# The left half of eight output chunks stored from GpSimd's queue, behind the last weights

## The chip, the core, the metric

The kernel runs on one core of a Trainium2 chip. The metric is device microseconds for one launch, median of several runs. PE is TensorE, DVE VectorE, ACT ScalarE, POOL GpSimd, and SP SyncE. DMA queue q0 takes what GpSimd issues, q1 what SP issues.

## The reference

Attention with four batches, eight heads, 768 positions and 64 features per head, some heads causal over everything, others with four sink positions and a window of 64. Its output, seen as 3072 rows of 512, goes into a mixture of eight experts with soft slots, four to an expert:

```python
logits = x @ phi                                  # 3072 x 32
d = softmax(logits, over rows)                    # dispatch
slot_input = (d.T @ x).reshape(8, 4, 512)
for e in range(8):
    slot_out[e] = relu(slot_input[e] @ w1[e]) @ w2[e]     # 512 -> 1024 -> 512
out = softmax(logits, over slots) @ slot_out      # 3072 x 512
```

All inputs and the output are float32; w1 and w2 are 2 MB for each expert.

## The kernel before

The program is one straight list of instructions. Attention runs over pairs of heads in an order written out by hand (ORDER), in which the loads of the weights are placed between the loads of q, k and v. All these loads are issued by GpSimd, since they cast float32 to bfloat16 on the way (w_load, w2_half). The second matrices of experts 5, 6 and 7 share their memory with the buffers of q, k, v and of the masks. So they come last, in halves of 256 output columns, left half (c = 0) and right half (c = 1), in this order:

```python
w_load(NE + 4)                 # expert 4, whole
w2_half(5, 0); w2_half(6, 0); w2_half(7, 0)
w2_half(5, 1); w2_half(6, 1); w2_half(7, 1)
```

After attention come the experts. `first` and `turn_h` make the hidden layer; `second(es, cols)` adds the products of the given experts for the left or right columns into one of two PSUM banks, `spb[0]` and `spb[1]` (L666). When the left bank is whole, VectorE scales it into the left half of `slot_out` (L742); ScalarE does the same for the right half (L751).

The 3072 output rows are twelve chunks of 256. For the first NL chunks the left half is computed before the right weights have come: `half_rows(i, 0)` makes two matmuls (L718), and evicts with VectorE (even chunks, L726) or with two ScalarE instructions (odd chunks, L724) into the tile `ot`, of which there are twelve buffers. `store` (L704) then issues a DMA on SP; for half a chunk it moves 256 KB in rows of 1 KB. When the right half of `slot_out` is there, `half_rows(i, 1)` follows for the NL chunks. The remaining chunks are made whole by `full_rows` (L734, L737, L739), with one store of 512 KB each.

`stir(c)` issues c matmuls of 128x448 whose result nobody reads (L678), so that TensorE has something to do while it waits for weights. TensorE takes its instructions in order, so that every product of `second` waits for the landing of its own weights and holds up what is behind it.

A DMA's issuing engine waits for the data that it moves, and for the earlier DMA that used the same completion count. There are eight such counts for GpSimd's DMAs and eight for SP's, used in turn.

Of the kernel before, what the change touches and what calls it, by code (L numbers as in the profile page):

```python
# [329 lines left out]
def kernel(  # L330
# [13 lines left out]
    nc = tc.nc  # L344
# [4 lines left out]
    NE, DM, F = moe_w1.shape  # L349
# [275 lines left out]
    def bank(i, shape, dt=F32):  # L625

        return tps.tile(shape, dt, tag=f"b{i}", name=f"b{i}")
# [28 lines left out]
    def second(es, cols, last=False):  # L656

        n = 4 // len(es)
        for c in cols:
            if c not in spb:  # L660
                spb[c] = bank(HP[6 + c], [P, 256])
        for f in range(8 // n):
            for x in range(4):
                e, fo = es[x // n], 8 // n * (x % n) + f
                for c in cols:
                    nc.tensor.matmul(spb[c][32 * x:32 * (x + 1), :], hTs[e // 4][:, fo, 32 * (e % 4):32 * (e % 4) + 32],  # L666
                                     w2s[e][:, fo, 256 * c:256 * (c + 1)],
                                     start=(x, c) not in begun, stop=last and f == 8 // n - 1)
                    begun.add((x, c))
# [3 lines left out]
    def stir(c):  # L673

        if not awake:
            awake.append(bank(HP[5], [P, 448]))
        for _ in range(c):
            nc.tensor.matmul(awake[0], ident, w1s[0][:, 0, :448], start=True, stop=True)  # L678
# [16 lines left out]
    second((7,), (0,), last=True)  # L695

    chunks = [(b, c) for b in range(B) for c in range(3)]
    NL = 7
    ots = {}

    def store(i, c0, c1):
        b, c = chunks[i]
        ov = out[b * S + 256 * c:b * S + 256 * (c + 1), :].rearrange("(p r) d -> p r d", r=2)
        nc.sync.dma_start(ov[:, :, c0:c1], ots[i][:, :, c0:c1])  # L704

    free = HP[:5]

# [4 lines left out]
    def half_rows(i, c):  # L712
        b, ch = chunks[i]
        if i not in ots:
            ots[i] = osb.tile([P, 2, DM], F32, tag="ot", name="ot")
        op = out_bank([P, 2, 256])
        for r in range(2):
            nc.tensor.matmul(op[:, r, :], out_rows(b, ch, r), slot_out[:, 256 * c:256 * (c + 1)],  # L718
                             start=True, stop=True)
        o = ots[i][:, :, 256 * c:256 * (c + 1)]  # L720
        rr = rrow[:, b, 2 * ch:2 * ch + 2]
        if i % 2:
            for r in range(2):
                nc.scalar.activation(o[:, r, :], op[:, r, :], ACT.Copy, scale=rr[:, r:r + 1])  # L724
        else:
            nc.vector.tensor_mul(o, op, rr.rearrange("p (r o) -> p r o", o=1).to_broadcast([P, 2, 256]))  # L726
        store(i, 256 * c, 256 * (c + 1))

    def full_rows(i):
        b, ch = chunks[i]  # L730
        ots[i] = osb.tile([P, 2, DM], F32, tag="ot", name="ot")
        for r in range(2):
            op = out_bank([P, 512])
            nc.tensor.matmul(op, out_rows(b, ch, r), slot_out, start=True, stop=True)  # L734
            rr = rrow[:, b, 2 * ch + r:2 * ch + r + 1]
            if r:
                nc.scalar.activation(ots[i][:, 1, :], op, ACT.Copy, scale=rr)  # L737
            else:
                nc.vector.tensor_scalar_mul(ots[i][:, 0, :], op, rr)  # L739
        store(i, 0, DM)  # L740

    nc.vector.tensor_scalar_mul(slot_out[:, :256], spb[0], rcol)  # L742
    for i in range(NL):
        if i == 4:
            second((5,), (1,))
        half_rows(i, 0)
        stir(1)
    second((6,), (1,))
    stir(4)
    second((7,), (1,), last=True)  # L750
    nc.scalar.activation(slot_out[:, 256:], spb[1], ACT.Copy, scale=rcol)  # L751
    for i in range(NL):
        half_rows(i, 1)
    for i in range(NL, len(chunks)):
        full_rows(i)
# [35 lines left out]
```

## Time and profile before

| | |
|---|---|
| median of 3 runs | 152.34 us (152.04 to 152.39) |
| the profiled execution's time | 152.27 us |
| its span, first to last instruction | 150.4 us |
| mean granted TensorE clock | 0.953 |
| busy: PE, DVE, ACT, POOL | 87%, 76%, 69%, 24% |
| q0 (GpSimd): packets, MB, share of 16 engines | 13104, 26.22, 92.8% |
| q1 (SP): packets, MB, share of 16 engines | 5248, 6.37, 12.2% |
| stores of half a chunk | 14 of 256 KB |
| stores of a whole chunk | 5 of 512 KB |

Times in the views are microseconds from the start of the span. In the rows of 40 digits each digit is a busy share in tenths for a fortieth of the span (or of the window asked for). The DMA share is that of the core's 16 DMA engines together; packets overlap, so it can be over 1. MB of q0 are counted as written, in bfloat16; twice as much is read. A matmul group's line gives its start, its length, and in brackets the idle time before it and what ended that.

### The profile page before, as it was taken

What the parts mean: (1) busy time and instruction counts of PE and PEld (TensorE: products, weight loads), DVE (VectorE), ACT (ScalarE), POOL (GpSimd) and SP (SyncE); (2) the same over time, 40 slices, a digit from 0 to 9 for tenths busy, and PEclk for the clock granted to TensorE, in tenths of its full rate; (3) what the DMA queues carried; (4) which work ended last, traced back from release to release, by engine and by line L of the source; (5) the groups of instructions that cost most, each with busy time, mean ns of one, the idle gap of its engine ahead of it and who ended that gap; (6) DMA issues with size and microseconds to landing.
All of it is one profiled execution on the core that took longest, in us unless ns stands there. A gap on an engine that the chain in (4) does not pass through costs nothing.

```text
span 150.4 us, 5249 instructions
## 1 busy us (share of the span) xinstructions
PE 130.2 (87%) x2321; PEld 84.1 (56%) x2321; DVE 114.7 (76%) x258; ACT 103.6 (69%) x139; POOL 36.2 (24%) x69
## 2 busy tenths in 40 slices
PE   6979999999999999999999999889799998439500
PEld 2436677676677677667757676556564745125100
DVE  4869899999969999998999998899933506208700
ACT  3029989999899999998989987999134104117700
POOL 6634231141137004025920000830530000000000
PEclk9999999999999999999999999999999999965955
DMA  2999999999999999999999999999999999975996
GB/s 24 200 207 208 209 228 201 215 227 201 211 224 203 216 224 196 227 207 203 227 212 213 222 216 216 213 211 218 220 206 192 198 199 197 300 263 187 356 403 251
DMA packets 18374, 32.91 MB, mean 219 GB/s; under 512 B 1712, under 2 KB 11440, under 8 KB 16688
## 3 DMA queue, kind: packets, MB, share of 16 engines
q0 software_dynamic: 13104, 26.22, 92.8%
q1 hardware_dynamic: 5248, 6.37, 12.2%
q8 instruction: 18, 0.29, 0.7%
q14 instruction: 4, 0.03, 0.1%
HBM read 52.50 MB, written 6.29 MB: 391 GB/s over the span
## 4 chain that ended last, share of the span: by engine, by line
PE 42%; DMA 20%; ACT 14%; DVE 13%; issue 2%; POOL 1%; POOLq 1%; ACTq 0%
DMA w<-in_moe_w_dram 16%; PE sc L166 11%; ACT pT L174 11%; PE pv L208 9%; DMA w<-in_k_dram 4%; DVE pT L193 4%; DVE xb L222 3%; PE tpv L120 3%; PE tpx L231 3%; PE tpk L120 3%; PE lgs L255 3%; PE tpq L120 2%; PE tpb L138 2%; PE b L718 2%; PE zp L422 1%
## 5 line engine op out<-in xcount | busy, mean ns | idle before, releaser
L174 ACT ACTIVATE pT<-sc 128x1024 bf16<-128x1024 f32 (+1 forms) x96 | 81.2, 928 | 5.4 <-PE sc L166 4.9
L193 DVE TENSOR_TENSOR pT<-pT,w 128x1024 bf16<-128x1024 bf16 (+2 forms) x64 | 33.0, 531 | 2.6 <-ACT pT L174 2.5
L166 PE MATMUL sc<-qT,kT 64*128 64x512 bf16 (+3 forms) x256 | 32.6, 309 | 1.7 <-ACT pT L174 1.0
L208 PEld LDWEIGHTS <-pT 128*128 128x128 bf16 x672 | 25.0, 97 | 9.5 <-issue 7.2
L208 PE MATMUL pv<-vb,pT 128*128 128x65 bf16 x352 | 28.5, 194 | 0.1
L120 PEld LDWEIGHTS <-w 96*64 96x64 bf16 x768 | 19.0, 111 | 9.6 <-issue 6.2
L208 PE MATMUL pv<-vf,pT 128*128 128x65 bf16 x320 | 24.3, 194 | 0.0
L222 DVE TENSOR_TENSOR xb<-pv,rs 128x768 bf16<-128x768 f32 (+1 forms) x17 | 15.5, 910 | 0.6
L166 PEld LDWEIGHTS <-kT 64*128 64x128 bf16 x256 | 10.4, 93 | 9.8 <-issue 3.7
L264 POOL COPY expT<-ep 128x128 bf16<-128x128 bf16 x18 | 6.8, 430 | 21.9 <-ACT ep L260 21.9
L724 ACT ACTIVATE ot<-b,rrow 128x256 f32<-128x256 f32 x12 | 5.0, 471 | 10.0 <-PE b L718 9.5
L726 DVE TENSOR_TENSOR ot<-b,rrow 128x512 f32<-128x512 f32 x8 | 5.5, 692 | 8.2 <-PE b L718 8.0
L153 DVE TENSOR_TENSOR vf<-vb,fmask 128x528 bf16<-128x528 bf16 x16 | 11.2, 697 | 0.0
L103 POOL DMA_DIRECT2D w<-in_k_dram x8 | 5.1, 643 | 19.3 <-PE sc L166 12.3
L422 PE MATMUL zp<-w 128*128 128x512 bf16 x23 | 8.5, 502 | 1.2 <-DVE quarter L425 1.2
L236 DVE COPY xT<-tpx 128x768 bf16<-128x768 bf16 x16 | 8.7, 549 | 0.7 <-PE tpx L231 0.7
L120 PE MATMUL tpk<-ident,w 96*64 96x96 bf16 x256 | 8.3, 208 | 1.0 <-DMA w<-in_k_dram 1.0
L231 PE MATMUL tpx<-ident,xb 128*128 128x128 bf16 x96 | 8.0, 218 | 1.0 <-DVE xb L222 0.8
L103 POOL DMA_DIRECT2D w<-in_q_dram x8 | 5.4, 672 | 14.1 <-PE tpq L120 13.2
L666 PE MATMUL b<-w,hT 128*32 128x256 bf16 x128 | 5.2, 283 | 3.9 <-DMA w<-in_moe_w_dram 3.9
L132 DVE COPY kT<-tpk 128x768 bf16<-128x768 bf16 x14 | 7.6, 549 | 1.2 <-PE tpk L120 1.2
L132 DVE COPY qT<-tpq 128x768 bf16<-128x768 bf16 x15 | 8.0, 549 | 0.7 <-PE tpq L120 0.7
(110 smaller groups left out, 168.5 us busy)
## 6 DMA issues: line engine op xcount, KB each, us to landing
w<-in_moe_w_dram POOLq DMA_DIRECT2D x13, 1024.0 KB, 17.9
out_dram<-ot SPq DMA_DIRECT2D x14, 256.0 KB, 4.8
w<-in_q_dram POOLq DMA_DIRECT2D x8, 384.0 KB, 12.4
w<-in_k_dram POOLq DMA_DIRECT2D x8, 384.0 KB, 10.5
w<-in_v_dram POOLq DMA_DIRECT2D x8, 384.0 KB, 10.9
w<-in_moe_w_dram POOLq DMA_DIRECT2D x6, 512.0 KB, 20.3
out_dram<-ot SPq DMA_DIRECT2D x5, 512.0 KB, 4.9
phf<-in_moe_phi_dram SPq DMA_DIRECT2D x4, 16.0 KB, 8.4
```

Of the source, the lines that this page charges most:

```text
L103: self.nc.gpsimd.dma_start(self.raws[t][Q % 2][:96], s)
L120: self.nc.tensor.transpose(tp[64 * hp:64 * hp + 64, x, :], raw[:96, hp, s * 64:s * 64 + 64], self.ident[:96, :96])
L132: self.nc.vector.tensor_copy(o, i)
L153: self.nc.vector.tensor_mul(vf, self.vbs[n // 2 % 2][:, n % 2, :, :4, :], fm.to_broadcast([128, 2, 4, VW]))
L166: nc.tensor.matmul(sc[:, hh, o:o + w], kT[ps, (g0 + j) * 128:(g0 + j + 1) * 128], qT[ps, g0 * 128 + q0:g0 * 128 + q0 + w], start=True, sto ...
L174: self.nc.scalar.activation(self.pT[n][:, :, lo:hi], self.sc.pop((n, u))[:, :, :hi - lo], ACT.Exp, scale=self.scale)
L193: nc.vector.tensor_mul(v, v, m)
L208: self.nc.tensor.matmul(pv[:, i * 65:(i + 1) * 65], pT[:, hh, o:o + 128], (vb if i - j <= 1 else vf)[:, j, :65], start=(j == 0), stop=(j = ...
L222: nc.vector.tensor_mul(x[:, hs], pv[:, :, :, :64], rs[:, :c].to_broadcast([128, c, 6, 64]))
L231: self.nc.tensor.transpose(tp[:, i * 128:(i + 1) * 128], self.xb[b][:, i, n4 * 128:(n4 + 1) * 128], self.ident)
L236: self.nc.vector.tensor_copy(self.xT[n // 4][:, n % 4], self.tp.pop(("x", n, 0)))
L422: nc.tensor.matmul(zp[:, i % 2, :], zw[:, :128], zw, start=True, stop=True)
```

## The change

Eight chunks instead of seven have their left half made ahead. Their left stores are issued by GpSimd and no longer by SP, after GpSimd's last weights; right halves and whole chunks stay on SP. So there are 8 left stores from GpSimd, and 8 right and 4 whole ones from SP. Four unread products are put ahead of expert 6's right product, and seven instead of four stand between it and expert 7's.

```diff
-    NL = 7
+    NL = 8
     ots = {}
 
     def store(i, c0, c1):
         b, c = chunks[i]
         ov = out[b * S + 256 * c:b * S + 256 * (c + 1), :].rearrange("(p r) d -> p r d", r=2)
-        nc.sync.dma_start(ov[:, :, c0:c1], ots[i][:, :, c0:c1])
+
+        (nc.gpsimd if c1 < DM else nc.sync).dma_start(ov[:, :, c0:c1], ots[i][:, :, c0:c1])
...
             second((5,), (1,))
         half_rows(i, 0)
         stir(1)
+    stir(4)
     second((6,), (1,))
-    stir(4)
+    stir(7)
     second((7,), (1,), last=True)
```

## The prediction

> **What bounds the kernel now.** I read the profile page first, then the chain that ended last, then the transfers and the busy times in short stretches of the last 30 us, since the change touches nothing before the left half of the output. On the page the DMA row is full to the end but for one hole, just where the clock row falls:
>
> ```profile
> PEclk9999999999999999999999999999999999965955
> DMA  2999999999999999999999999999999999975996
> GB/s 24 200 207 208 209 228 201 215 227 201 211 224 203 216 224 196 227 207 203 227 212 213 222 216 216 213 211 218 220 206 192 198 199 197 300 263 187 356 403 251
> ```
>
> The chain of waits says who stands around that hole (start, length, what):
>
> ```profile
> 109.44 24.01 DMA w<-in_moe_w_dram
> 133.49 0.64 PE b L666 x7
> 134.16 0.48 ACT slot_out L751
> 134.68 3.14 PE b L718 x14
> ```
>
> The last weights, right half of expert 7's second matrix, were issued at 109.44 and landed at 133.45. Only then come the product, the right half of slot_out, and the right stores. The left stores, which need none of this, are issued by SP from 125.98 on. The busy times by stretch, whose last columns are the clock, the DMA share and GB/s, show what that does:
>
> ```profile
> 126.00:128.00 2.00, 2.00 (x22) 1.12 (x19) 1.36 (x2) 1.53 (x5) 0.00 (x0) 1.00 1.46 198
> 130.00:132.00 2.00, 0.37 (x2) 0.09 (x1) 0.00 (x0) 0.00 (x0) 0.00 (x0) 1.00 1.12 351
> 132.00:133.50 1.50, 0.01 (x3) 0.01 (x2) 0.00 (x0) 0.00 (x0) 0.00 (x0) 0.85 0.95 325
> 133.50:135.00 1.50, 0.93 (x10) 0.48 (x10) 0.00 (x0) 0.47 (x1) 0.00 (x0) 0.50 0.62 220
> 135.00:136.00 1.00, 1.00 (x7) 0.67 (x5) 0.69 (x1) 0.27 (x1) 0.00 (x0) 0.50 0.20 70
> 136.00:137.00 1.00, 1.00 (x7) 0.67 (x6) 0.69 (x1) 0.99 (x4) 0.00 (x0) 0.50 0.04 15
> 145.00:149.20 4.20, 0.00 (x0) 0.00 (x0) 0.00 (x0) 0.00 (x0) 0.00 (x0) 0.50 0.97 383
> ```
>
> Three things are to be seen. The DMA engines, full until 133, run dry before the first right store arrives. Taking 1.00 as full, the idle part is 0.05 x 1.5 + 0.38 x 1.5 + 0.80 + 0.96, and half of 137.0 to 137.5: 2.64 us of all 16 engines. They don't run dry together: a share of 0.20 is three engines, 0.04 less than one. And from 137.2 to the last packet at 149.2 they are full again, so the end is set by bytes. Besides, the stores squeeze the weights; the queues from 131 to 132 (packets, MB, share):
>
> ```profile
> q1 hardware_dynamic: 369, 0.36, 104.9%
> q0 software_dynamic: 11, 0.01, 4.1%
> ```
>
> q0, the GpSimd queue, still has a trickle of weights on a few late engines, while q1, SP's, has the rest. On the late engines stores and weights take turns, and the right product waits for the latest.
>
> **The change part by part.** The sum is made against the profiled execution: span 150.4, time 152.27, so 1.87 lies around the span; the median is 152.34, 0.07 more.
>
> *Weights first.* The eight left stores (c1 is 256, under DM) go into q0 behind all weights. Expert 6's right half landed at 129.1 (the wait before its product ended at 129.11), when stores had hardly begun. A half is 0.52 MB, at 198 GB/s 2.65 us. So expert 7's lands at about 131.75 instead of 133.45: 1.7 us earlier.
>
> *From landing to the first right store.* Before: 133.49 to 136.02, SP's issue, and first packets at 137.2, 3.7 us. Expert 7's product took 0.62 and the first output pair, to its eviction, 0.62 too (134.68 to 135.30), in a stretch with clock 0.50; at clock 1.00 the left ones took 0.40 and 0.41 (124.85 to 125.26). That saves 0.4 if TensorE stays awake, so first right packets at 131.75 + 3.3 = 135.05. These 2.1 us are worth only what the DMA queues leave of them.
>
> *Unread products.* The eighth left chunk adds a pair and one unread product, 0.41 by the step of its neighbours; four unread products took 0.86, seven make 1.43. From 128.23, where TensorE was done with seven chunks: 128.64, 129.50 after four, 129.85 after expert 6's right product (landed at 129.1, so 0.4 late, which nobody waits for), 131.3 after seven. Expert 7 lands at 131.75: cost nothing. If it landed at 130.7, they would cost 0.6 on the right product, still behind left stores. The bound is 0 to 0.6; I take 0.
>
> *GpSimd's issues.* GpSimd has no work after 110.3. Its issues took 0.54 to 0.90, SP's 0.58; eight follow the evictions, from 126.0 on. The order of the changed kernel shows more: each store takes the next of eight completion counts, so stores 6, 7 and 8 also wait for the right halves of experts 5, 6 and 7. The first two have landed by then. The eighth can be issued at 131.75 only, and with 0.9 of issue and 1.2 until packets (SP's 136.02 to 137.2) starts at 133.9. At 126.0 q0 had 1359 packets of weights left, which at the 386 a us of 120 to 124 are gone by 129.5 on the mean engine; seven stores of 0.70 then last to 134.4, so it isn't missed; only behind an early engine is there a gap. Nothing is queued on GpSimd behind it.
>
> The Trainium skill, "DMA: Bandwidth & Descriptors", section "SWDGE vs HWDGE vs iDMA", speaks against this: GpSimd writes its descriptors into SBUF, where VectorE in its two-port mode locks it out. By that the issues could stretch. The trace of before doesn't show it: two weight issues at 72.82 took 1.08 together while VectorE was over nine tenths busy.
>
> *Rate of the stores in q0.* The trace has no store there. From above: q1's 1 KB packets, 370 in a us on 16 engines, 43 ns each, up to 46.5 with all busy (344 GB/s, 138 to 140): 0.69 to 0.75 a store, 16 packets an engine. From below: the weights' packets also read 1 KB, 1024 in 2.65 us on 16 engines, 41 ns. The worst row is the time of one q0 packet from 120 to 124: 143.9% of 16 engines x 4 us over 1545 packets is 59.6 ns, but these overlap. I take 0.70 a store, the range 0.66 to 0.95.
>
> *SP.* Seven issues leave its queue, and one 512 KB store becomes two of 256 KB, one on each queue. A full store costs 1.29 (0.524 MB at 405 GB/s, 143.5 to 149), a half one on SP 0.76 (0.262 MB at 344): two halves 0.70 + 0.76, 0.17 more.
>
> *The sum.* If all engines fill their hole, 2.64 - 0.17 = 2.5 us are won. The latest engine has less to win: its left packets ended at about 136.55 (where the share goes to zero), so it was idle for 0.65. It then has the eighth left store, 0.70, until 137.25, eight right ones of 0.76 and four full of 1.29: 148.5. Before, the last packets were at 149.2. That is 0.7 won. Why it is late: expert 7's left half landed at 122.74 (issued 106.84, 15.9 to landing); two halves later is 128.04, but expert 6's right half landed at 129.1, 1.06 late. Between them, before 124, q8 fetched instructions once; q8's 18 packets with 0.7% of 16 engines x 150.4 us are 0.94 us each, on one engine. Before, the hole absorbed this lateness; now it doesn't. But a late engine works while others have finished, at 43 ns a packet, not 46.5: 8 x 16 x 3.5 ns = 0.4 of the right stores. I take 1.1, nearer to the latest engine than to the mean: every store needs all 16. Time: 152.27 - 1.1 = 151.2.
>
> **The rivals.** *Engines even out* (0.17): lateness is recovered, since early engines idle while late ones catch up. For it: 4% and 20% in the hole are few engines; against it: the late one's 1.06 at 129.1 is more than one whole fetch. 152.27 - 2.5 = 149.8.
>
> *Order without gain* (0.13): weights and stores interleave as before and expert 7 still lands at 133.45. Left stores then end before 137.2 on most engines all the same, and only the eighth chunk's half is won: after 137.2 eight x 0.76 + four x 1.29 instead of seven and five, 0.53 less: 151.7. Against it: from 115 to 126, with weights alone, q0 ran at an even 198 GB/s in order. The Trainium skill says in the same page, "Issuing engines are not separate DMA queues", that choosing another issuing engine only saves issue time; by that alone I would have said 0 won. The same page, "Queues, rings and completion order", has rings of one queue taken in order, which is what the rest of my case needs.
>
> *Slower* (0.14): q0's store packets take the whole 59.6 ns instead of 43. Eight stores x 16 packets x 16.6 ns = 2.1 us, on every engine, between the weights and the right stores, so nothing hides it: 152.27 - 1.1 + 2.1 = 153.3. It decides from 43 + 1100 / 128 = 52 ns a packet. For it: the row stands there; against it: the same row moves a packet each 41 ns. A late issue on GpSimd would have the same sign, but needs stores 3 us late.
>
> **How the numbers follow.** Forecast 0.56, the three rivals 0.44. This kernel can be told from no change at 0.3%, 0.46 us. Faster takes most of the forecast (0.48; the rest falls within, as its own bounds are 150.6 to 151.9), the evened case (0.17) and some of the third (0.05): 0.70. Within: 0.16. Slower: 0.14. The range reaches from 150.0, short of the evened end, to 152.6, into the slow case.
>
> **What would show it.** Right: expert 7's wait ends near 131.75; the DMA share stays about 1 from 130 to 149; q1 starts at about 135; the chain names stores and not weights; the last packets near 148.1, spread over engines. Wrong: a share under 0.9 between 131 and 136 (stores issued late or slow); left stores landing more than 0.8 apart in q0; expert 7 landing at 133 or later; unread products standing right before its product.

## The result, and the profile after

The changed kernel took 151.39 us (median of 20 runs, 150.72 to 152.84) against 152.36 for the kernel before (20 runs): ratio 0.9955, 95% interval 0.9933 to 0.9976. That is 0.97 us by the medians, 0.36 to 1.02 by the interval; forecast were 151.2 and 1.1.

The profiled execution of the changed kernel was one of the long ones (152.84, span 151.1), and it was long before the change begins: VectorE scaled the left half of slot_out at 126.20, against 124.31 in before. So times of the two profiles are not laid side by side here; I count from landmarks, events that both traces have. The chain of waits of the changed kernel (start, length, what):

```profile
111.32 22.78 DMA w<-in_moe_w_dram
...
134.14 0.42 PE b L666 x8
...
134.59 0.48 ACT slot_out L753
...
135.12 0.61 PE b L719 x4
```

From the left scaling to the end of the wait for expert 7's right weights it is 7.94 us, where it was 9.18. The busy times by stretch (the last three columns are the clock, the DMA share, GB/s):

```profile
132.00:133.50 1.50, 1.12 (x6) 0.48 (x5) 0.00 (x0) 0.00 (x0) 1.16 (x2) 1.00 1.08 348
133.50:135.00 1.50, 0.40 (x8) 0.22 (x8) 0.00 (x0) 0.41 (x1) 0.35 (x1) 1.00 1.01 379
135.00:136.00 1.00, 0.88 (x9) 0.79 (x9) 0.47 (x1) 0.32 (x2) 0.33 (x1) 1.00 0.79 303
136.00:137.00 1.00, 1.00 (x10) 0.68 (x8) 1.00 (x3) 1.00 (x4) 0.00 (x0) 1.00 0.74 275
137.00:137.50 0.50, 0.38 (x4) 0.18 (x2) 0.50 (x2) 0.50 (x2) 0.00 (x0) 1.00 0.25 98
145.00:149.20 4.20, 0.00 (x0) 0.00 (x0) 0.00 (x0) 0.00 (x0) 0.00 (x0) 0.50 0.93 370
```

The hole in the DMA share is smaller, 0.21 + 0.26 + 0.75 x 0.5 = 0.85 us of 16 engines instead of 2.64, but it is not closed. GpSimd's and SP's issues in the timeline (start, length, and in brackets the idle time before and what ended it):

```profile
128.14 5.02 POOL L705 DMA_DIRECT2D out_dram<-ot  x7 [15.95 <-DVE ot L727]
134.65 0.69 POOL L705 DMA_DIRECT2D out_dram<-ot  x1 [1.49 <-DMA w<-in_moe_w_dram]
136.25 9.37 SPq L705 DMA_DIRECT2D out_dram<-ot  x12
```

The eighth left store did wait 1.49 for the weights, as the order of completion counts said. SP's first right store came 2.11 after the end of expert 7's wait, where it was 2.53. Last, what GpSimd's stores look like on the queue: q0 had 13104 packets before.

```profile
q0 software_dynamic: 13744, 28.31, 96.8%
q1 hardware_dynamic: 3472, 4.27, 8.2%
```

640 packets more for eight stores are 80 each, for 256 KB: 64 of 4 KB and 16 short ones, not 1 KB rows one by one as on q1.

One thing stood in no term of the forecast. From the last landing to the end of the span it was 0.91 in before, 1.35 here. The waits of SP (line, what it waited for: total, times, longest), in before and then in the changed kernel:

```profile
SPq L786 <- DMA out_dram<-ot: 3.2, 3, 1.2
```

```profile
SPq L788 <- DMA out_dram<-ot: 4.0, 1, 4.0
```

At the end SP goes through its completion counts one after the other, in a fixed order, some 0.06 us each even when they are full (in the changed kernel's trace its last waits follow the last landing at steps of 0.06 us). In before the last three stores end three waits in turn, and the last store's count is the last in the order. With 12 stores on SP instead of 19 the last store falls on the first of the eight counts: one wait of 4.0, and all the others still to be gone through behind the last landing.

### The profile page after: what moved, and what is told of

Same layout as the page of the kernel before. It is cut to its first block, busy times and chain, and to the rows that moved or that the text cites. A ratio compares the mean times of both kernels' runs of the same rounds, so it can differ in the third digit from the quotient of the medians.

```text
span 151.1 us, 5272 instructions
## 1 busy us (share of the span) xinstructions
PE 129.4 (86%) x2329; PEld 84.1 (56%) x2331; DVE 113.6 (75%) x257; ACT 104.0 (69%) x142; POOL 42.0 (28%) x77
## 4 chain that ended last, share of the span: by engine, by line
PE 47%; DMA 20%; ACT 19%; DVE 3%; issue 3%; POOL 2%; ACTq 0%; POOLq 0%
DMA w<-in_moe_w_dram 15%; PE sc L166 14%; ACT pT L174 13%; PE pv L208 11%; DMA w<-in_k_dram 5%; PE tpv L120 4%; PE tpx L231 3%; PE tpq L120 3%; PE tpk L120 3%; PE tpb L138 3%; PE lgs L255 3%; ACT ot L725 2%; PE zp L422 2%; DVE xb L222 1%; ACT ot L738 1%
## 5 line engine op out<-in xcount | busy, mean ns | idle before, releaser
L208 PEld LDWEIGHTS <-pT 128*128 128x128 bf16 x672 | 24.9, 97 | 9.3 <-issue 7.1
L725 ACT ACTIVATE ot<-b,rrow 128x256 f32<-128x256 f32 x16 | 6.3, 480 | 9.5 <-PE b L719 9.1
L705 POOL DMA_DIRECT2D out_dram<-ot x8 | 5.7, 1081 | 17.4 <-DVE ot L727 15.9
L120 PE MATMUL tpq<-ident,w 96*64 96x96 bf16 x256 | 8.1, 209 | 1.0 <-DMA w<-in_q_dram 1.0
L120 PE MATMUL tpv<-ident,w 96*64 96x96 bf16 x256 | 8.7, 216 | 0.0
## 6 DMA issues: line engine op xcount, KB each, us to landing
w<-in_moe_w_dram POOLq DMA_DIRECT2D x13, 1024.0 KB, 16.9
```

Of the source, the lines that this page charges most:

```text
L120: self.nc.tensor.transpose(tp[64 * hp:64 * hp + 64, x, :], raw[:96, hp, s * 64:s * 64 + 64], self.ident[:96, :96])
L208: self.nc.tensor.matmul(pv[:, i * 65:(i + 1) * 65], pT[:, hh, o:o + 128], (vb if i - j <= 1 else vf)[:, j, :65], start=(j == 0), stop=(j = ...
```

## The experiments

To compare executions that reach the end at different times, I use one more landmark of each trace: the mean of the 16 engines' landings of expert 7's left half, which no store touches. "Wait" is from there to the end of the wait for expert 7's right half, "rest" from the end of that wait to the end of the span, "SP" from it to SP's first right store, "last" from the last landing to the end. "Stage", in the texts below, is from VectorE's scaling of the left half of slot_out to the end of the span: 26.1 in before, 24.9 in the changed kernel. The trace gives the 16 landings of each DMA without the engines' names; "the latest engine" is the last of the 16.

| kernel | time, us | ratio (95%) | wait | rest | SP | last |
|---|---|---|---|---|---|---|
| before | 152.36 | | 11.74 | 16.96 | 2.53 | 0.91 |
| after | 151.39 | 0.9955 (0.9933 to 0.9976) | 10.52 | 16.92 | 2.11 | 1.35 |
| a_all_on_sp | 151.95 | 0.9994 (0.9969 to 1.0019) | 12.08 | 16.45 | 2.11 | 1.35 |
| b_seven_left | 151.21 | 0.9958 (0.9935 to 0.9982) | 10.72 | 17.03 | 2.11 | 1.34 |
| c_stir_as_before | 150.88 | 0.9935 (0.9914 to 0.9956) | 10.58 | 16.92 | 2.53 | 1.34 |
| d_last_count | 150.48 | 0.9906 (0.9878 to 0.9934) | 10.63 | 16.33 | 2.11 | 0.91 |
| e_eighth_on_sp | 150.71 | 0.9877 (0.9840 to 0.9915) | 9.79 | 16.45 | 2.11 | 0.92 |
| f_queue_only | 151.11 | 0.9907 (0.9878 to 0.9935) | 10.45 | 17.04 | 2.11 | 1.34 |
| g_count_stir | 150.33 | 0.9856 (0.9826 to 0.9887) | 10.59 | 16.34 | 2.32 | 0.91 |
| h_right_on_gpsimd | 151.35 | 0.9922 (0.9894 to 0.9950) | 10.68 | 17.18 | | 0.91 |
| i_queue_and_count | 151.17 | 0.9951 (0.9920 to 0.9982) | 10.12 | 16.63 | 2.11 | 0.91 |
| j_eighth_stir | 151.07 | 0.9939 (0.9905 to 0.9974) | | | | |

a to d, e to h, and the last two shared runs of the kernel before, which gave 152.12, 152.56 and 152.08; so times and ratios of different groups can differ by 0.3% without meaning anything.

**a_all_on_sp**

```diff
-        (nc.gpsimd if c1 < DM else nc.sync).dma_start(ov[:, :, c0:c1], ots[i][:, :, c0:c1])
+        nc.sync.dma_start(ov[:, :, c0:c1], ots[i][:, :, c0:c1])
```

> Edit: as the changed kernel (eight left halves, four and seven unread products), but all stores are issued by SP again. I measure from the start of VectorE's scaling of the left half of slot_out to the end of the span, as the attention stage before it varies by 1 to 2 us between executions: 26.09 in the kernel before, 24.90 in the changed kernel. Expert 7's right weights end their wait 9.18 after that start in before, 7.94 in after. Theory (order of queues): stores take turns with weights again, so the wait ends at 9.2 to 9.6 and the stage takes 25.6 to 26.2; the time is within 0.3% of before. Rival (the eighth chunk and the unread products make the gain): the wait still ends late but the stage stays at 24.9 to 25.2, and the ratio near 0.995.

The wait ended 9.47 after the left scaling, the stage took 25.9, the time is that of before. Without the queue no gain is left in the time. That doesn't mean that the other two parts do nothing: the rest is 0.51 shorter than in before, although the end behind the last landing is 0.44 longer; the wait is 0.34 longer. All stores on SP, with that end as in before, was not run.

**b_seven_left**

```diff
-    NL = 8
+    NL = 7
```

> Edit: as the changed kernel, but seven left halves, all issued by GpSimd. Theory (the queue makes the gain, the eighth half only fills): the weights land as in the changed kernel (wait ends 7.9 to 8.1 after the left scaling starts); one more whole store after the right ones start adds up to 0.53, but no left store waits for the last weights any more: stage 24.9 to 25.4. Rival (the eighth store, which can only be issued once expert 7's weights have landed, costs more than it brings): stage under 24.8.

The weights landed as in the changed kernel (7.98 after the left scaling), stage 25.0, time 0.9958: as the theory had it. The eighth half is not what makes the gain. That its late issue costs more than it brings is not borne out: the stage would have been under 24.8.

**c_stir_as_before**

```diff
-    stir(4)
     second((6,), (1,))
-    stir(7)
+    stir(4)
```

> Edit: as the changed kernel, but with the unread products of before (none ahead of expert 6's right product, four behind it). Theory: TensorE falls to half clock and the way from the weights' landing to SP's first right store takes 2.5 instead of 2.1 us; the early engines feel it, the latest one has left stores until then, so the end moves by 0 to 0.4: stage 24.9 to 25.3. Rival (the unread products make the gain): stage 25.6 or more. Second rival (they are in the way): stage 24.6 or less.

Stage 25.2, in the theory's range; the time, 150.88, is not above the changed kernel's. The product of expert 7 in the PE timeline, in the changed kernel, here, and in f_queue_only, which has the same unread products as this one (start, length, in brackets the idle time before):

```profile
134.14 0.40 PE L666 MATMUL b<-w,hT 128*32 128x256 bf16 x8 [1.02 <-DMA w<-in_moe_w_dram]
```

```profile
132.16 0.62 PE L666 MATMUL b<-w,hT 128*32 128x256 bf16 x8 [1.82 <-DMA w<-in_moe_w_dram]
```

```profile
132.22 0.40 PE L666 MATMUL b<-w,hT 128*32 128x256 bf16 x8 [1.78 <-DMA w<-in_moe_w_dram]
```

With the same idle time of 1.8 us the clock had fallen in one execution (granted 0.50 in the stretch from 132.0 to 133.5) and not in the other (1.00). With four unread products behind expert 6's product it had fallen before expert 7's in this profile, and not in those of f_queue_only, g_count_stir, i_queue_and_count and j_eighth_stir; with eleven (the changed kernel, a, b, d, e, h) it was 1.00 in that stretch in every profile. Where it fell, the 0.42 until SP's first right store did not show at the end.

**d_last_count**

```diff
-            for qh in range(2):
-                nc.sync.dma_start(phf[64 * hp:64 * hp + 64, 2 * qh:2 * qh + 2, :],
-                                  moe_phi.rearrange("(qh hp a d) s -> qh hp d a s", qh=2, hp=2, a=2)[qh, hp])
+            for c in range(4):
+                at_row = 256 * (c // 2) + 128 * hp + 64 * (c % 2)
+                n = 2 if 4 * hp + c < 3 else 1
+                for x in range(n):
+                    w = 64 // n
+                    nc.sync.dma_start(phf[64 * hp + w * x:64 * hp + w * x + w, c, :],
+                                      moe_phi[at_row + w * x:at_row + w * x + w, :])
```

> Edit: as the changed kernel, but phi is loaded in eleven small DMAs on SP instead of four, early and long before it is used, so that the last whole store uses the last of SP's eight completion counts and not the first. Theory: at the end SP waits for its counts one after the other, about 0.063 us each even if all are full; in the changed kernel the last store's count is the first of eight, so some 0.45 us of waits come behind the last landing (last landing to end 1.38, against 0.87 in before). With the last store on the last count the end comes 0.40 to 0.45 sooner: stage 24.4 to 24.5, ratio to before near 0.9925. Rival (those waits lie beside the landing, the late end is something else): stage 24.9, ratio 0.9955.

From the last landing to the end it is 0.91 again, the stage is 24.25, a little under the theory's 24.4, and the time is the best of its group. SP's final waits:

```profile
SPq L792 <- DMA out_dram<-ot: 3.4, 3, 1.2
```

Three waits as in before, where the changed kernel had one of 4.0. This is shown: the place of the last store in the order of counts is worth 0.44 us.

**e_eighth_on_sp**: d_last_count, and

```diff
-        (nc.gpsimd if c1 < DM else nc.sync).dma_start(ov[:, :, c0:c1], ots[i][:, :, c0:c1])
+        (nc.gpsimd if c1 < DM and i < 7 else nc.sync).dma_start(ov[:, :, c0:c1], ots[i][:, :, c0:c1])
```

> Edit: as d_last_count (last store on the last completion count; phi in ten pieces instead of eleven keeps that so), but the eighth left store is issued by SP, so that no left store waits for expert 7's weights. Theory: in d_last_count GpSimd issues it at 132.7 and the DMA share falls to 0.80 (133.5 to 135.0) and 0.49 (135 to 136); issued from SP at about 130 it fills some of that, but takes turns with the last weights on the late engines, whose wait ends 0 to 0.7 later than 132.3: the two cancel within 0.3%, span 148.4 to 149.0 (148.7 in d_last_count). Rival (the late issue is what is lost): span 148.2 or less. Rival (any store ahead of the weights costs its whole length): 149.2 or more.

```profile
133.50:135.00 1.50, 0.93 (x15) 0.75 (x8) 0.30 (x1) 0.56 (x2) 0.00 (x0) 1.00 1.02 378
135.00:136.00 1.00, 1.00 (x9) 0.70 (x8) 1.00 (x3) 1.00 (x4) 0.00 (x0) 1.00 1.00 368
136.00:137.00 1.00, 0.88 (x6) 0.40 (x5) 1.00 (x2) 1.00 (x4) 0.00 (x0) 1.00 0.84 312
```

The hole is all but closed: 0.16 us of 16 engines from 132.0 to 137.0, against 0.84 in d_last_count. That the eighth store's late issue had left it open is not shown by this: the wait is 0.84 shorter than in d_last_count as well, for no reason that these runs show, and a shorter wait alone narrows the hole. The span of 149.8 lies where the second rival has it (149.2 or more), but this execution was 1.8 us late before the stores (its left half of expert 7 landed at 123.5 on the mean engine, 121.7 in d_last_count), and its wait was not longer, as that rival needs. Whether the edit shortens the kernel stays open: wait and rest together are 26.24 against 26.96, the median is 150.71 against 150.48 in another group, and the times, 150.22 to 151.60, overlap those of d_last_count, 150.27 to 150.82.

**f_queue_only**: the kernel before with the store's line alone changed.

```diff
-        nc.sync.dma_start(ov[:, :, c0:c1], ots[i][:, :, c0:c1])
+        (nc.gpsimd if c1 < DM else nc.sync).dma_start(ov[:, :, c0:c1], ots[i][:, :, c0:c1])
```

> Edit: the kernel before with one line changed: its seven left stores are issued by GpSimd; the unread products are those of before. Theory (the order in the queue is the gain): expert 7's wait ends at 132.1 to 132.4 as in b_seven_left and c_stir_as_before (133.49 in before, 133.70 in a_all_on_sp), and the span is 149.1 to 149.8, ratio 0.994 to 0.998. Rival (queue, eighth half and unread products are needed together): wait ends after 133, span 150.0 or more.

Its chain of waits:

```profile
109.36 22.82 DMA w<-in_moe_w_dram
...
132.22 0.43 PE b L666 x8
```

The weights were issued when they were in before (109.44) and their wait ended at 132.22 instead of 133.49. What stands in front of them shows in the landing of the first left store, issued at 125.98 in before and at 126.31 here (the store, its size, us from issue to landing on all engines; before first):

```profile
out_dram<-ot SPq DMA_DIRECT2D x1, 256.0 KB, 6.6
```

```profile
out_dram<-ot POOLq DMA_DIRECT2D x1, 256.0 KB, 6.5
```

In before this store was down at 132.54, 0.91 ahead of the last weights; here at 132.78, 0.61 behind them (132.17). Span 149.3, and a ratio lower than I expected, in the group with the highest median of before. Wait and rest together are 27.49, in the changed kernel 27.44: one line brings as much as the whole change.

**g_count_stir**: d_last_count with the unread products of before (c_stir_as_before's edit).

> Edit: d_last_count with the unread products of before (none and four). Theory: SP's first right store comes 0.4 later, the end does not move, since by then most engines still have left stores and the rest is bytes: span 148.5 to 148.9, ratio 0.989 to 0.992. Rival (awake TensorE is worth its 0.4 when the tail is out of the way): span 149.0 or more, ratio 0.993 or more.

Span 148.5, 150.33 us, the lowest median of all; the ratio is below what I expected, in the same group with the highest median of before. The unread products of the change can go.

**h_right_on_gpsimd**: d_last_count, and

```diff
-        (nc.gpsimd if c1 < DM else nc.sync).dma_start(ov[:, :, c0:c1], ots[i][:, :, c0:c1])
+        (nc.gpsimd if c1 - c0 < DM else nc.sync).dma_start(ov[:, :, c0:c1], ots[i][:, :, c0:c1])
```

> Edit: d_last_count, but the right halves are issued by GpSimd too; only the four whole chunks stay on SP, whose last one is on the last count again. Theory (seen in the profile of after: eight left stores added 640 packets to q0, 80 each, while one on q1 takes 256 and more; they land 0.65 to 0.70 apart, right ones from SP 0.76): GpSimd's stores travel in packets of 4 KB, so eight right ones take 0.5 to 0.9 less, against 0.5 more until the first packets: span 147.9 to 148.7, ratio 0.985 to 0.991. Rival (the packets change nothing, and GpSimd issues slower than SP and waits for its counts): span 149.0 or more.

The rival's span came: 149.6 against 148.7 in d_last_count, and 0.9 more time, in another group. All transfers from 140 to 145, here (first line, then its queues) and in d_last_count (second fence):

```profile
DMA packets 505, 1.77 MB, mean 355 GB/s; under 512 B 72, under 2 KB 72, under 8 KB 505
...
q1 hardware_dynamic: 282, 1.02, 56.8%
q0 software_dynamic: 223, 0.75, 43.2%
```

```profile
DMA packets 1043, 1.95 MB, mean 389 GB/s; under 512 B 82, under 2 KB 730, under 8 KB 1043
```

The right halves did travel in few large packets, but with both queues at work on large packets 355 GB/s came out, and SP alone with many small ones among its packets moved 389. Nor is it the size: from 141 to 144, where f_queue_only has almost only packets of 4 KB from SP, it moved 408, and the two queues here 358. Besides, GpSimd stood 1.19 and 0.43 before two of its issues, and the hole from 132 to 137 is 1.27 us of 16 engines, 0.84 in d_last_count. Large packets were no gain here; why the mixture is slower was not tried.

**i_queue_and_count**: f_queue_only with d_last_count's edit of phi.

> Edit: the kernel before with two changes only: its seven left stores are issued by GpSimd, and phi is loaded in eleven pieces, so that the last store is on SP's last completion count. Theory (the two effects add): f_queue_only took 151.11 with the last store on the first count; 0.44 less is 150.67, and the last landing is 0.9 before the end, not 1.35; expert 7's wait ends near 132.2. Rival (the late count hides under something when the right stores come later): 150.9 or more. What is left to d_last_count (150.48) and g_count_stir (150.33) is then what the eighth left half is worth: 0.2 to 0.35.

The time missed: 151.17 (150.64 to 152.40) is where the rival has it. Its profile speaks against the rival: last landing to end 0.91, and the rest 16.63 instead of 17.04, 0.41 less where 0.44 was expected, so the late count did not hide under anything. Why the time did not follow is open; in the profile the left half of expert 7 landed 0.5 later than in f_queue_only.

**j_eighth_stir**: e_eighth_on_sp with the unread products of before.

> Edit: as e_eighth_on_sp, with the unread products of before (none and four). Theory: in e_eighth_on_sp the DMA share from 132 to 137 was 1.06, 1.02, 1.00 and 0.84, so the bytes set the end and TensorE's clock does not: the usual execution stays at 150.2 to 150.6, within 0.3% of g_count_stir (150.33). Rival (with full queues the right product is what the end waits for): 150.8 or more.

151.07 (150.33 to 152.64) is on the rival's side, 150.8 or more, but so wide a spread settles nothing. In its profile the left half of expert 7 landed 2.6 later than in d_last_count, so I don't read it. Open.

## Why the prediction was right

The time, the sign and the size came out, and so did the step that everything hung on. That the number came so close is partly luck: 1.1 was a choice between the bounds 0.7 and 2.5, the weights came 0.45 less early than forecast, and a loss of 0.44 at the end stood in no term. By the landmarks, the span after the mean landing went from 28.70 to 27.44, 1.26 less, and the table gives the parts:

- *Weights first*, the step that everything hung on: the wait is 1.22 shorter (11.74 to 10.52; f_queue_only 1.29, a_all_on_sp none). Forecast were 1.7. The direction is shown; the size was too high by about 0.45, since the latest engine's weights came later than a half's length, 2.65, after expert 6's: 3.05 in f_queue_only, 3.50 in the changed kernel. An instruction fetch falls into that stretch in these profiles (q8 from 131 to 132 in the changed kernel); that it was on that engine is argued, not shown.
- *Landing to first right store*: 0.42 won, forecast 0.4. That it takes more unread products is not so: f_queue_only had it with the old ones, and c_stir_as_before did not.
- *Unread products at no cost*: right; TensorE still stood 1.02 before expert 7's product.
- *GpSimd's issues*: right about the counts that each store waits for. The first engine had the seventh left store down at 135.68, the eighth at 136.97, which is 1.29 later where a store takes 0.65, and the first right one at 138.58: the rest of the hole lies on both sides of the eighth store. The gap ahead of it I gave to early engines alone and priced at nothing; no run shows time won by closing it.
- *Rate in q0*: 0.70 a store was taken; on the latest engine the last seven each landed 0.63 to 0.66 after the one before. The price was near, its reason wrong: large packets, not fast small ones. That ends the slower rival (59.6 ns a packet of 1 KB).
- *SP's queue*: one whole store less and one half more behind the first right store, 0.53 by the prediction's prices; the rests of f_queue_only and a_all_on_sp, seven left halves and eight with the same "SP" and "last", are 0.59 apart. Its seven fewer DMAs I counted as nothing, and there the forecast failed: they moved the last store onto the first count, 0.44 at the end (d_last_count).
- *The latest engine*: I gave it most of the say, and took 1.1 instead of 2.5. In the changed kernel it landed the last store 0.42 behind the one before it, in d_last_count 0.22. With seven left stores (b, f, i) it was 0.03 or less, but in c_stir_as_before and g_count_stir, which have eight, 0.02 or less too. There the right stores came 0.2 to 0.4 later, so that the late engine had longer to catch up; that this is the reason is argued. So in the changed kernel the late engine takes back what the earlier right stores had won.

The parts add up: 1.22 + 0.42 + 0.53 - 0.44 - 0.42 = 1.31, against 1.26. They do so for the experiments too. Starting from before's rest of 16.96, a_all_on_sp has 0.42 off for SP, 0.53 off for the whole store and 0.44 on for the count: 16.45, as measured; f_queue_only 16.98, measured 17.04; c_stir_as_before 16.87, measured 16.92; i_queue_and_count 16.54, measured 16.63. With its latest engine's 0.22, d_last_count gets 16.23, measured 16.33; g_count_stir, 0.21 off for SP and 0.53 for the store, 16.22, measured 16.34.

So the change moved the last weights forward, and the end went with them: it comes 16.9 us after their wait in both kernels. That these two rests are alike is luck, 0.95 won against 0.86 lost; in the experiments the rest goes from 16.33 to 17.18. Of my signs, expert 7's wait came near its mark: 134.14, less the 1.89 by which this execution was late, is 132.25, and I had said 131.75. The left stores were no more than 0.66 apart. Others failed: the chain still names the weights (15% of the span) and not the stores, the DMA share fell to 0.79 and 0.74 instead of staying about 1, and the last packets were not spread evenly over the engines. The hole in the DMA share, from which I derived the bounds, was smaller because the weights came earlier, but it did not close as the upper bound needs. *Order without gain* fell with f_queue_only and a_all_on_sp: which queue a store is put into decided 1.2 us, where the Trainium skill ("DMA: Bandwidth & Descriptors", "Issuing engines are not separate DMA queues") counts only issue time; what the trace agrees with is the order within a ring, in "Queues, rings and completion order" of the same page. *Engines even out* was half right: they did in f_queue_only (0.03 between the last two landings), but the 2.5 us did not follow, since the engines then waited for the right stores.

Of the change's three parts, the queue brings the gain, and the unread products bring nothing that these runs can tell (c_stir_as_before, g_count_stir). What the eighth half is worth is open: with the last store on the first count the rest is 16.92 with eight (the changed kernel, c) and 17.03 with seven (b, f has 17.04); on the last count it is 16.33 and 16.34 with eight (d, g) and 16.63 with seven (i), 0.3 less, but no group of runs has both kinds there. Where one has, c took 150.88 and b 151.21, and these differ in the unread products too. d_last_count and g_count_stir, with the last store back on the last count, have lower medians than both kernels: 150.48 and 150.33.

## What to carry to other kernels

Try to put transfers that nobody waits for into the same queue behind the one that is waited for; on another queue they took turns with it here, which cost the weights 1.2 us. When DMAs move between queues, recount which completion count each one gets: a store may inherit a wait for the very load that it should fill in for (1.49 here), and the last one may leave a row of finished waits behind it (0.44 here). A sum that comes out can still hold two wrong terms: each term needs its own landmark in the profile after.

## What the runs showed of the hardware

A store of 256 KB in rows of 1 KB left GpSimd's queue in 64 packets of 4 KB and 16 short ones; from SP each row was a packet. Large packets on both queues at once moved 358 GB/s (h_right_on_gpsimd, 141 to 144), less than the 408 from SP alone (f_queue_only). SP took 0.06 us for each count that was full already, 0.44 in all. TensorE's granted clock fell within 1.8 us of idling in one execution (c_stir_as_before) and not in another (f_queue_only).
